# Tap sums by accumulating transfers into device memory, and token products in another order, in a softmax-convolution and mixer kernel

## The chip, the cores and the metric

The kernel runs on one core of one Trainium2 chip. The metric is device time in microseconds (us) of one launch. TensorE is written PE, VectorE DVE, ScalarE ACT, GpSimd POOL and SyncE SP. A change of 0.2% (4.7 us) is about what a measurement of this kernel can tell from none.

## The reference

Two stages in float32. The first is a causal convolution of seven taps whose weights are a softmax per position and head; the second is a mixer with two token products and two channel products for each of eight batches.

```python
w = softmax(weight_gen, axis=-1)                  # (8, 4096, 8 heads, 7 taps), 1e-9 in the divisor
xa[b, s, h, :] = sum_k w[b, s, h, k] * x_pad[b, s + k, h, :]      # d_model 192 = 8 heads x 24
h1 = relu(xa^T @ w_tok1)                          # over the 4096 positions, to 256
u  = xa + (h1 @ w_tok2)^T                         # back to 4096 positions
out = u + relu(u @ w_ch1) @ w_ch2                 # 192 -> 1536 -> 192
```

The weights come in as doubles, and products are kept near float32 by splitting operands in a high and a low part.

## The kernel before

A batch of 4096 positions is cut in eight chunks of 512, each held as 128 partitions x 4 x 192 elements (384 KB); there are 64 chunks, counted m or g. A prologue converts the first weights and does the tap sums of batch 0. The loop at L797 then takes one chunk g at a time through the two channel products, in six steps p. A step is ten matmuls into a `ph` bank (`channel1`, L488), the ReLU on ACT and the low part on DVE (`h`, L499, L500), and, two steps behind, sixteen matmul pairs into `acc` (`channel2`, L504). `ph`, `th` and `up` share two buffers of PSUM (`ps_w`).

Between steps stand the products over tokens. `token1` (L388) sums chunk m of the *next* batch into `h1s`; eight of them make that batch's h1. `token2_half` (L437) runs twice per chunk and gives `ur`, which `columns_of` (L462) transposes on DVE, moves with 24 copies on ACT and splits (L424 to L429) into the operands that the next chunk's first step reads. `store` (L521) adds `acc` to `ur` on DVE and writes the chunk out through POOL's queue.

The tap sums of the batches from 1 on run on DVE beside this. `attention` (L188) does one chunk at a time: product k=0 straight into `xa`, then six products into `pr` (two buffers) and six adds into `xa`. Nine buffers of `xa` (`RING`) keep each sum in SBUF from there until `token2_half`, eight chunks later.

The order of everything is written out when the program is built, by a small planner. It keeps a clock per engine (`at`), holds chains of pending items with costs, and `pump` issues what fits before the next `h` is due. `attention_stream` is one such chain; `token1_ready` and the `if` at L820 to L827 decide which token product stands behind which step. Engines then run in the written order.

```python
        yield "v", cost, first
        yield "v", cost, lambda: one(1)
        for k in range(2, K):
            yield "v", cost, lambda k=k: one(k)
            yield "v", cost, lambda k=k: add(k - 1)
        yield "v", cost, lambda: add(K - 1)
```

Of the kernel before, what the change touches and what calls it, by code (L numbers as in the profile page):

```python
# [21 lines left out]
def mixer_kernel(ctx: ExitStack, tc: tile.TileContext, x, wg, wt1, wt2, wc1, wc2, out):  # L22
# [17 lines left out]
    RING = NCH + 1  # L40
    F1, F2 = 2, 2
    LAG = 2
    SM = 2

# [27 lines left out]
    def load_x(m):  # L72

        b, i = divmod(m, NCH)
        t = p1.tile([P, CT + PAD, D], F32, tag="xt", name="xt", bufs=3)
# [98 lines left out]
    xat, xht = {}, {}  # L174
# [9 lines left out]
    def new_xa(m):  # L184
        xat[m] = p1.tile([P, CT, D], F32, tag="xa", name="xa", bufs=RING)
        return xat[m]

    def attention(m):  # L188
        box = {}
        NE = CT * D  # L190
        cost = 70 + NE * 1.05

        def first():
            box["src"], (box["wn"], box["j"]) = xt.pop(m), wnt.pop(m)
            box["acc"] = new_xa(m)
            mul(box["acc"], 0)

        def mul(dst, k):
            x_k, w = taps(box["src"], box["wn"], box["j"], k, k + 1)
            nc.vector.tensor_mul(  # L200
                dst.rearrange("p t (h g) -> p (t h) g", h=H).rearrange("p (o n) g -> p o n g", o=1), x_k, w)

        def one(k):
            box[k] = late.tile([P, CT, D], F32, tag="pr", name="pr", bufs=2)
            mul(box[k], k)

        def add(k):
            nc.vector.tensor_add(box["acc"], box["acc"], box.pop(k))  # L208
        yield "v", cost, first
        yield "v", cost, lambda: one(1)  # L210
        for k in range(2, K):
            yield "v", cost, lambda k=k: one(k)
            yield "v", cost, lambda k=k: add(k - 1)
        yield "v", cost, lambda: add(K - 1)

    def two_parts(m):
# [12 lines left out]
        yield "n", 0, lambda: ready.append((m, max(at["dve"], at["act"]) + HOP))  # L229
# [14 lines left out]
    def sums(m, prs):  # L244
        acc = new_xa(m)
# [7 lines left out]
        for n in range(2):  # L253
            nc.scalar.copy(acc[:, n * half:(n + 1) * half, :], ps[:, n, 0:half * D])

# [11 lines left out]
    def load_w1(m):  # L267
# [26 lines left out]
    def convert_w2(i):  # L294
# [7 lines left out]
        def last():  # L302
# [3 lines left out]
            nc.gpsimd.dma_start(s2[i], t)  # L306
        yield "a", 950, last

    def load_w2(m):
# [5 lines left out]
        else:  # L315
# [6 lines left out]
            if b == F2:  # L322
                v = v.rearrange("p (k n) -> p k n", k=KR)
                yield from split(t[:, :, 0], t[:, :, 1], v)
                yield "n", 0, lambda: nc.gpsimd.dma_start(s3[i], flat)
# [111 lines left out]
    def token2_half(m, half):  # L437

        b, i = divmod(m, NCH)
        xa, h1, w = xat[m], h1t[b], w2t[m]  # L440
# [18 lines left out]
        if half == 1:  # L459
            del xat[m], w2t[m]  # L460
# [74 lines left out]
    at = {"pe": 0.0, "act": 0.0, "dve": 0.0}  # L535
    HOP = 60
    AFTER = 130
    LOAD = 5000
    SOON = 500
# [4 lines left out]
    FIRST = 0  # L544
# [3 lines left out]
    free = {"acc": 0.0, "u": 0.0}  # L548
    ready = deque()
# [5 lines left out]
    class Chain:  # L555
# [14 lines left out]
        def issue(self):  # L570
            kind, cost, fn = self.item
            fn()
# [12 lines left out]
    def pump(limit):  # L585

        scalar = not state["rush"] and any(c.item is not None and c.item[0] == "u" for c in chains)
        while True:
            best = None
            for c in chains[1:] + chains[:1]:  # L590
# [11 lines left out]
                if kind in "as" and c.wait > max(at["act"], at["pe"]):  # L602
                    continue
# [6 lines left out]
                if kind in "an":  # L610
# [25 lines left out]
    EARLY = 12  # L636
# [11 lines left out]
    def prefetch(m):  # L648

        if m >= NG:  # L650
            return
# [15 lines left out]
    def attention_stream():  # L667
        for m in range(NCH, NG):
            prefetch(m + AHEAD)
            if m % SM == 0 and m > NCH:  # L670
                yield from softmax(m)
            yield "gate", 0, lambda: m - RING <= state["token2"]
            yield from attention(m)
            yield "n", 0, lambda: add_chain(two_parts(m), at["dve"] + HOP)

    with tc.tile_pool(name="pro", bufs=1) as pro:
# [29 lines left out]
        for m in range(NCH):  # L706
            prs = products(m, pro)
            prefetch(m + AHEAD)
# [27 lines left out]
            v_old = v  # L736
        token1_first(NCH - 1, v)
# [13 lines left out]
    stream = chain(softmax(NCH), attention_stream())  # L751
# [5 lines left out]
    run(last, w2_it, islice(stream, EARLY))  # L757
# [20 lines left out]
    def do_token2(m):  # L778
# [10 lines left out]
        state["token2"] = m  # L789
        if NCH <= m + 1 < NG:  # L790
# [6 lines left out]
    for g in range(NG + 1):  # L797
        parts = None if g + 1 < NG else iter(())
        state["rush"] = g == 0
# [70 lines left out]
```

## Time and profile before

| | |
|---|---|
| three runs | 2343.65, 2344.04 (median), 2345.75 us |
| profiled execution | 2343.91 us; its span 2342.1 us |
| busy | PE 2196.7 us (94%), DVE 1842.1 (79%), ACT 1085.0 (46%), POOL 58.4 (2%) |
| tap sums on DVE | 392 products and 336 adds of 128x768 |
| DMA | 244.69 MB, 104 GB/s over the span |

Busy time on PE counts matmuls that overlap, so a busy PE is not PE at its peak. Every chunk ends in one store on POOL (L532), so the distance between two stores is the time of a chunk. The loop over chunks begins at about 130 us; chunks 0 to 7 are batch 0, and so on.

### The profile page before, as it was taken

What the parts mean: (1) busy time and instruction counts of PE and PEld (TensorE: products, weight loads), DVE (VectorE), ACT (ScalarE), POOL (GpSimd) and SP (SyncE); (2) the same over time, 40 slices, a digit from 0 to 9 for tenths busy, and PEclk for the clock granted to TensorE, in tenths of its full rate; (3) what the DMA queues carried; (4) which work ended last, traced back from release to release, by engine and by line L of the source; (5) the groups of instructions that cost most, each with busy time, mean ns of one, the idle gap of its engine ahead of it and who ended that gap; (6) DMA issues with size and microseconds to landing.
All of it is one profiled execution on the core that took longest, in us unless ns stands there. A gap on an engine that the chain in (4) does not pass through costs nothing.

```text
span 2342.1 us, 30675 instructions
## 1 busy us (share of the span) xinstructions
PE 2196.7 (94%) x12256; PEld 1962.0 (84%) x12256; DVE 1842.1 (79%) x2231; ACT 1085.0 (46%) x2265; POOL 58.4 (2%) x104
## 2 busy tenths in 40 slices
PE   7869989999998999999999999999999999999998
PEld 5558878888887888888888888888888888899997
DVE  8889887878876888879887888869887798844443
ACT  4675443544534355345434434444443454344443
POOL 0000000000000000000000000000000000000000
PEclk9989999999999999999999999999999999999999
DMA  7733131223241333313332232332233132211110
GB/s 282 233 133 140 63 106 70 100 97 114 92 156 62 108 113 135 120 64 124 123 107 99 105 122 80 116 112 104 101 107 120 63 124 103 73 55 46 46 42 21
DMA packets 52127, 244.69 MB, mean 104 GB/s; under 512 B 6008, under 2 KB 15736, under 8 KB 38672
## 3 DMA queue, kind: packets, MB, share of 16 engines
q1 hardware_dynamic: 43360, 196.58, 24.3%
q0 software_dynamic: 8624, 46.14, 4.9%
q8 instruction: 97, 1.59, 0.3%
q14 instruction: 46, 0.38, 0.0%
HBM read 192.36 MB, written 50.33 MB: 104 GB/s over the span
## 4 chain that ended last, share of the span: by engine, by line
PE 38%; ACT 19%; DVE 14%; issue 11%; DMA 1%; POOL 0%; POOLq 0%; ACTq 0%; SPq 0%; DVEq 0%
PE ph L496 17%; ACT a_f L476 9%; PE acc L514 9%; ACT c_f L476 4%; PE acc L516 4%; ACT h L499 4%; DVE h L500 3%; DVE xa L208 3%; PE th L397 3%; DVE pr L200 3%; PE up L449 2%; DVE uc L429 1%; PE th L398 1%; DVE a_lo L426 1%; DMA w<-s 1%
## 5 line engine op out<-in xcount | busy, mean ns | idle before, releaser
L514 PE MATMUL acc<-w2s,h 128*128 128x384 f32 x3072 | 902.1, 358 | 0.0
L499 ACT ACTIVATE h<-ph 128x1024 fp32r<-128x1024 f32 x384 | 392.8, 1023 | 1004.4 <-PE ph L496 980.3
L516 PE MATMUL acc<-w2s,h 128*128 128x192 f32 x3072 | 773.5, 252 | 0.0
L500 DVE SCALAR_TENSOR_TENSOR h<-ph,h 128x1024 fp32r<-128x1024 f32 x384 | 468.3, 1220 | 294.3 <-ACT h L499 292.7
L516 PEld LDWEIGHTS acc<-w2s,h 128*128 128x128 f32 x3072 | 591.3, 192 | 16.0
L514 PEld LDWEIGHTS acc<-w2s,h 128*128 128x128 f32 x3072 | 583.3, 190 | 16.0
L496 PE MATMUL ph<-a_hi,w1a_hi 128*128 128x512 f32 x768 | 321.6, 419 | 58.9 <-ACT a_hi L424 33.9
L496 PE MATMUL ph<-uc,w1c_hi 128*128 128x512 f32 x768 | 311.7, 406 | 44.2 <-DVE uc L429 44.2
L200 DVE TENSOR_TENSOR pr<-xt,wn 128x768 f32<-128x768 f32 x336 | 318.2, 952 | 4.1
L208 DVE TENSOR_TENSOR xa<-xa,pr 128x768 f32<-128x768 f32 x336 | 319.7, 952 | 1.0
L496 PE MATMUL ph<-a_lo,w1a_hi 128*128 128x512 f32 x768 | 306.8, 399 | 6.0 <-DVE a_lo L426 6.0
L476 ACT COPY a_f<-t 32x128 f32<-32x128 f32 x1024 | 302.6, 295 | 16.6 <-DVE t L468 5.5
L496 PE MATMUL ph<-a_hi,w1a_lo 128*128 128x512 f32 x768 | 305.6, 398 | 0.0
L496 PE MATMUL ph<-uc,w1c_lo 128*128 128x512 f32 x768 | 305.2, 397 | 0.0
L496 PEld LDWEIGHTS ph<-uc,w1c_hi 128*128 128x128 f32 x768 | 146.6, 191 | 97.6 <-DVE uc L429 49.4
L496 PEld LDWEIGHTS ph<-a_hi,w1a_hi 128*128 128x128 f32 x768 | 146.5, 191 | 87.4 <-ACT a_hi L424 37.3
L496 PEld LDWEIGHTS ph<-a_lo,w1a_hi 128*128 128x128 f32 x768 | 146.6, 191 | 45.8 <-DVE a_lo L426 14.4
L496 PEld LDWEIGHTS ph<-uc,w1c_lo 128*128 128x128 f32 x768 | 147.4, 192 | 30.1
L496 PEld LDWEIGHTS ph<-a_hi,w1a_lo 128*128 128x128 f32 x768 | 148.0, 193 | 16.0
L476 ACT COPY c_f<-t 32x128 f32<-32x128 f32 x512 | 152.0, 297 | 7.4
L528 DVE TENSOR_TENSOR ur<-acc,ur 128x384 f32<-128x384 f32 x256 | 136.2, 553 | 8.3 <-PE acc L516 3.9
L449 PE MATMUL up<-h,w 128*128 128x384 f32 x384 | 116.4, 359 | 0.0
(70 smaller groups left out, 1914.8 us busy)
## 6 DMA issues: line engine op xcount, KB each, us to landing
w<-s SPq DMA_DIRECT2D x80, 1024.0 KB
xt<-in_x_dram SPq DMA_DIRECT2D x56, 960.0 KB
out_dram<-ur POOLq DMA_DIRECT2D x63, 384.0 KB, 4.9
raw<-in_moe_w_tok_dram SPq DMA_DIRECT2D x16, 1024.0 KB
s<-w POOLq DMA_DIRECT2D x16, 1024.0 KB, 4.1
val<-s SPq DMA_DIRECT2D x24, 512.0 KB
wg<-in_weight_gen_dram SPq DMA_DIRECT2D x64, 112.0 KB
s<-val SPq DMA_DIRECT2D x8, 512.0 KB
```

The costliest lines, as they stand in the source:

```text
L200: nc.vector.tensor_mul(dst.rearrange("p t (h g) -> p (t h) g", h=H).rearrange("p (o n) g -> p o n g", o=1), x_k, w)
L208: nc.vector.tensor_add(box["acc"], box["acc"], box.pop(k))
L397: nc.tensor.matmul(th[:, r, 0:2 * D], w[:, c, 0, rs], xh[:, c, :], start=c == 0, stop=False)
L398: nc.tensor.matmul(th[:, r, 0:D], w[:, c, 1, rs], xh[:, c, 0:D], start=False, stop=c == CT - 1)
L449: nc.tensor.matmul(up[:, j, 0:2 * D], w[:, k, 0, cs], h1[:, k, :], start=k == 0, stop=False)
L476: nc.scalar.copy(dst[to:to + Q, :].rearrange("p (c n j) -> p c n j", c=CT, n=NQ)[:, :, n, :], box["t"][n * Q:(n + 1) * Q, :, d, :])
L496: nc.tensor.matmul(ph[:, j, :], w[:, fs], u, start=n == 0, stop=n == len(steps) - 1)
L499: nc.scalar.activation(h[:, :, 0, :], ph, AF.Relu)
L500: nc.vector.scalar_tensor_tensor(h[:, :, 1, :], ph, 0.0, h[:, :, 0, :].bitcast(F32), op0=ALU.max, op1=ALU.subtract)
L514: nc.tensor.matmul(ps[:, 0:2 * D], h[:, j, 0, cs], w2s[:, f, :], start=f == 0, stop=False, **kw)
L516: nc.tensor.matmul(ps[:, 0:D], h[:, j, 1, cs], w2s[:, f, 0:D], start=False, stop=f == NF - 1, **kw)
L528: nc.vector.tensor_add(u[:, t, :], a[:, :, l * D:(l + 1) * D], u[:, t, :])
```

## The change

The six adds per chunk leave DVE. All seven products of a chunk go to `pr` tiles, now eight of them, and each is sent by a DMA on POOL's queue to a tile `xs` in device memory: the first writes, the other six add to what is there (`accum_op`). Two chunks are done in turn, product by product, so that the transfer of one is under way while the other's is issued. The sum is then loaded twice through SP: as `xa` (two buffers) for `token1`, and later as `xb` (two buffers) for `token2_half`. The prologue's sums for chunks 2 to 7 are also written out and loaded again. The 23 later stores of converted weights (to `s2`, `s1`, `s3`) move from POOL's queue to SP's. The x of a pair is loaded when the pair before has had its last product. The planner gets a clock for POOL, and the `if` of the main loop now prefers the halves of token2 to token1.

```diff
-    RING = NCH + 1
+    RUN = NCH + 3
+    PR = 8
...
+    def keep(m):
+        xst[m] = dram.tile([P, CT * D], F32, name=f"xs{m}")
+        return xst[m]
+
+    def load_xa(m):
+
+        xbt[m] = p1.tile([P, CT, D], F32, tag="xb", name="xb", bufs=2)
+        nc.sync.dma_start(xbt[m].rearrange("p t d -> p (t d)"), xst.pop(m))
+
+    def attention(ms):
...
+        def one(m, k):
+            t = late.tile([P, CT, D], F32, tag="pr", name="pr", bufs=PR)
+            x_k, w = taps(xt[m], *wnt[m], k, k + 1)
             nc.vector.tensor_mul(
...
+        def add(m, k):
+            if k == 0:
+                nc.gpsimd.dma_start(keep(m), prt.pop((m, k)))
+            else:
+                nc.gpsimd.dma_start(xst[m], prt.pop((m, k)), accum_op=ALU.add)
+            done[m] = on("pool", ISSUE, at["dve"] + HOP, done.get(m, 0.0)) + ADD
+            pr_free.append(done[m])
+
+        def fetch(m):
+            nc.sync.dma_start(new_xa(m).rearrange("p t d -> p (t d)"), xst[m])
+            xa_at[m] = max(at["pe"], at["dve"]) + FETCH
+            add_chain(two_parts(m), xa_at[m])
...
+        for k in range(K):
+            for m in ms:
+                yield "w", 0, lambda: pr_free.popleft()
+                yield "v", cost, lambda m=m, k=k: one(m, k)
+                yield "n", 0, lambda m=m, k=k: add(m, k)
...
-        xa, h1, w = xat[m], h1t[b], w2t[m]
+        xa, h1, w = xbt[m], h1t[b], w2t[m]
...
-            yield "n", 0, lambda: nc.gpsimd.dma_start(s1[i], flat)
+            yield "n", 0, lambda: nc.sync.dma_start(s1[i], flat)
...
+            yield "gate", 0, lambda: m + SM - 1 - RUN <= state["token2"]
+            yield "w", 0, lambda: x_at[m]
+            yield from attention(range(m, m + SM))
+            if m + SM < NG:
+                yield "t", 0, lambda: load_pair(m + SM)
...
-            if token1_ready() and (p == LAG - 1 or ready[0][0] < g + NCH + ((g + 1) % NCH == 0)):
+            last = (g + 1) % NCH == 0 and (g + 1) // NCH not in h1t and g + 1 < NG
+            if token1_ready() and last:
                 do_token1()
-            elif parts is not None:
+            elif parts is not None and len(halves) > 0:
+                halves.pop()
                 next(parts, None)
-            elif p >= FIRST and g + 1 in w2t and (g + 1) // NCH in h1t \
-                    and max(w_at[0], h1_at[(g + 1) // NCH]) <= at["pe"]:
+            elif parts is None and g + 1 in w2t and (g + 1) // NCH in h1t \
+                    and max(w_at[0], h1_at[(g + 1) // NCH]) <= at["pe"] + 300:
                 parts = do_token2(g + 1)
                 next(parts)
+                halves.append(1)
+            elif token1_ready() and ready[0][0] <= g + NCH:
+                do_token1()
```

**DVE, an inner chunk of batch 3, before.** `ur<-up` is what follows a half of token2, `h1s<-th` what follows token1, `h` closes a step, `ur<-acc` is the store of the chunk before.

```order
L456 TENSOR_TENSOR ur<-up,xa 128x384
L458 TENSOR_TENSOR ur<-up,ur 128x384
L500 SCALAR_TENSOR_TENSOR h<-ph,h 128x2x512
L528 TENSOR_TENSOR ur<-acc,ur 128x384 x4
L406 TENSOR_TENSOR h1s<-th,h1s 128x384
L408 TENSOR_TENSOR h1s<-th,h1s 128x384
L225 TENSOR_TENSOR xh<-xa,xh 128x4x192
L500 SCALAR_TENSOR_TENSOR h<-ph,h 128x2x512
L456 TENSOR_TENSOR ur<-up,xa 128x384
L458 TENSOR_TENSOR ur<-up,ur 128x384
L468 STREAM_TRANSPOSE t<-ur 128x768
```

The same chunk as changed (lines are 27 higher there; `pr<-xt,wn` are tap products, which follow in groups of up to four with no add between):

```order
L483 TENSOR_TENSOR ur<-up,xb 128x384
L485 TENSOR_TENSOR ur<-up,ur 128x384
L527 SCALAR_TENSOR_TENSOR h<-ph,h 128x2x512
L555 TENSOR_TENSOR ur<-acc,ur 128x384 x4
L483 TENSOR_TENSOR ur<-up,xb 128x384
L485 TENSOR_TENSOR ur<-up,ur 128x384
L495 STREAM_TRANSPOSE t<-ur 128x768
L209 TENSOR_TENSOR pr<-xt,wn 128x768
L527 SCALAR_TENSOR_TENSOR h<-ph,h 128x2x512
L209 TENSOR_TENSOR pr<-xt,wn 128x768 x4
L433 TENSOR_TENSOR h1s<-th,h1s 128x384
L435 TENSOR_TENSOR h1s<-th,h1s 128x384
```

The second half of token2 and the transpose stand one step and a token1 earlier. The pair's other nine products follow behind this chunk's next three `h`, three at a time: four `h` stand between the first and the last of the fourteen.

**DVE, the end of a batch (chunk 31), before.** Two token1 stand in it, one with the ReLU of h1 (L385):

```order
L208 TENSOR_TENSOR xa<-xa,pr 128x768
L406 TENSOR_TENSOR h1s<-th,h1s 128x384
L408 TENSOR_TENSOR h1s<-th,h1s 128x384
L385 SCALAR_TENSOR_TENSOR h_9907<-h1s,h_9907 128x2x192
L225 TENSOR_TENSOR xh<-xa,xh 128x4x192
L500 SCALAR_TENSOR_TENSOR h<-ph,h 128x2x512
L528 TENSOR_TENSOR ur<-acc,ur 128x384 x4
L408 TENSOR_TENSOR h1s<-th,h1s 128x384
L500 SCALAR_TENSOR_TENSOR h<-ph,h 128x2x512
L456 TENSOR_TENSOR ur<-up,xa 128x384
L458 TENSOR_TENSOR ur<-up,ur 128x384
L500 SCALAR_TENSOR_TENSOR h<-ph,h 128x2x512
```

As changed:

```order
L247 TENSOR_TENSOR xh<-xa,xh 128x4x192
L433 TENSOR_TENSOR h1s<-th,h1s 128x384
L435 TENSOR_TENSOR h1s<-th,h1s 128x384
L412 SCALAR_TENSOR_TENSOR h_10152<-h1s,h_10152 128x2x192
L527 SCALAR_TENSOR_TENSOR h<-ph,h 128x2x512
L555 TENSOR_TENSOR ur<-acc,ur 128x384 x4
L483 TENSOR_TENSOR ur<-up,xb 128x384
L485 TENSOR_TENSOR ur<-up,ur 128x384
L527 SCALAR_TENSOR_TENSOR h<-ph,h 128x2x512
L483 TENSOR_TENSOR ur<-up,xb 128x384
L485 TENSOR_TENSOR ur<-up,ur 128x384
L495 STREAM_TRANSPOSE t<-ur 128x768
```

The second token1 has left this chunk, and token2 stands one step earlier.

**POOL, a pair of chunks as changed** (before, this queue held a store per chunk here and nothing else). `xs_6513` and `xs_6568` are the two sums.

```order
L559 DMA out_dram<-ur 128x768 x2
L217 DMA xs_6513<-pr 128x768
L217 DMA xs_6568<-pr 128x768
L219 DMA xs_6513<-pr 128x768
L219 DMA xs_6568<-pr 128x768
L219 DMA xs_6513<-pr 128x768
L219 DMA xs_6568<-pr 128x768
L219 DMA xs_6513<-pr 128x768
L219 DMA xs_6568<-pr 128x768
```

Three more such pairs of rows follow. Each row of L219 waits until the one before it on the same sum has landed.

## Rows read from the trace of the kernel before

**Rows 1.** The page: busy us, share of the span and instructions of each engine.

```profile
PE 2196.7 (94%) x12256; PEld 1962.0 (84%) x12256; DVE 1842.1 (79%) x2231; ACT 1085.0 (46%) x2265; POOL 58.4 (2%) x104
```

**Rows 2.** The page: the chain that ended last, by engine.

```profile
PE 38%; ACT 19%; DVE 14%; issue 11%; DMA 1%; POOL 0%; POOLq 0%; ACTq 0%; SPq 0%; DVEq 0%
```

**Rows 3.** Timeline of POOL, one store per chunk: start, us, what [idle before].

```profile
184.84 0.56 POOL L532 DMA_DIRECT2D out_dram<-ur  x1 [15.04 <-PE ph L496]
...
440.20 0.54 POOL L532 DMA_DIRECT2D out_dram<-ur  x1 [27.14 <-DVE ur L528]
...
812.27 0.55 POOL L532 DMA_DIRECT2D out_dram<-ur  x1 [16.52 <-DVE ur L528]
...
1056.03 0.54 POOL L532 DMA_DIRECT2D out_dram<-ur  x1 [32.02 <-DVE ur L528]
...
1255.94 0.54 POOL L532 DMA_DIRECT2D out_dram<-ur  x1 [33.09 <-DVE ur L528]
...
1329.11 0.54 POOL L532 DMA_DIRECT2D out_dram<-ur  x1 [32.03 <-DVE ur L528]
...
2041.58 0.54 POOL L532 DMA_DIRECT2D out_dram<-ur  x1 [32.90 <-DVE ur L528]
...
2164.49 0.54 POOL L532 DMA_DIRECT2D out_dram<-ur  x1 [29.04 <-DVE ur L528]
...
2282.78 0.54 POOL L532 DMA_DIRECT2D out_dram<-ur  x1 [29.03 <-DVE ur L528]
```

**Rows 4.** Waits of PE over the span: us in total, times, longest us.

```profile
PE ph L496 <- DVE uc L429: 44.2, 54, 2.3
PE ph L496 <- ACT a_hi L424: 33.9, 12, 9.7
PE ph L496 <- DVE h L500: 24.6, 28, 7.0
```

**Rows 5.** Windows: us, busy of PE, PEld, DVE, ACT, POOL, PE clock, DMA, GB/s.

```profile
1155.40:1188.90 33.50, 32.50 (x190) 29.43 (x189) 29.10 (x38) 14.97 (x34) 0.57 (x2) 1.00 0.29 104
1280.00:1286.00 6.00, 5.34 (x13) 3.81 (x14) 2.15 (x3) 0.76 (x2) 0.00 (x0) 0.50 0.01 3
```

**Rows 6.** The chain in order of time, one step and a half of token2.

```profile
1155.22 2.33 PE ph L496 x10
...
1159.80 0.20 PE up L449
...
1160.94 2.31 PE ph L496 x10
```

**Rows 7.** Timeline of PE in batch 0: token1, and a half of token2.

```profile
172.93 2.79 PE L415 MATMUL th<-xa,val 128*128 128x192 f32 x16
...
176.17 0.50 PE L496 MATMUL ph<-a_hi,w1a_hi 128*128 128x512 f32 x1 [0.46 <-DVE h L500]
...
180.82 1.49 PE L447 MATMUL up<-h,w 128*128 128x192 f32 x8
...
182.18 0.50 PE L496 MATMUL ph<-a_hi,w1a_hi 128*128 128x512 f32 x1
```

**Rows 8.** Groups by line: busy us, mean ns of one, idle before.

```profile
L200 DVE TENSOR_TENSOR pr<-xt,wn 128x768 f32<-128x768 f32 x336 | 318.2, 952 | 4.1
L208 DVE TENSOR_TENSOR xa<-xa,pr 128x768 f32<-128x768 f32 x336 | 319.7, 952 | 1.0
```

**Rows 9.** DMA queues over the span: packets, MB, share of 16 engines.

```profile
q1 hardware_dynamic: 43360, 196.58, 24.3%
q0 software_dynamic: 8624, 46.14, 4.9%
```

**Rows 10.** The stores of L532: issue on POOL in ns, and landing.

```profile
L532 POOL DMA_DIRECT2D out_dram<-ur x63: 539/539/556, 184.8 to 2311.2; - x63
...
DMA to landing us min/median/max: 2.6/4.9/8.8
```

**Rows 11.** Waits: DVE for the high part in a weight split.

```profile
DVE w L150 <- ACT w L149: 24.0, 12, 5.3
```

More of the change, by code (lines that the diff above doesn't have):

```diff
@@ L74, in load_x @@
         b, i = divmod(m, NCH)
-        t = p1.tile([P, CT + PAD, D], F32, tag="xt", name="xt", bufs=3)
+        if m < NCH and m % 3 == 2:
+            t = pro.tile([P, CT + PAD, D], F32, tag="xt", name="xt")
+        else:
+            t = p1.tile([P, CT + PAD, D], F32, tag="xt", name="xt", bufs=2)
         xt[m] = t
@@ L184, in new_xa @@
     def new_xa(m):
-        xat[m] = p1.tile([P, CT, D], F32, tag="xa", name="xa", bufs=RING)
+        xat[m] = p1.tile([P, CT, D], F32, tag="xa", name="xa", bufs=2)
         return xat[m]
[L188 to L199, printed above, removed]
-            nc.vector.tensor_mul(
[L201 to L214, printed above, removed]
+    def keep(m):
+        xst[m] = dram.tile([P, CT * D], F32, name=f"xs{m}")
+        return xst[m]
@@ L571, in issue @@
             kind, cost, fn = self.item
+            if kind == "w":
+                self.wait = max(self.wait, fn())
+                self.next()
+                return
             fn()
@@ L601, in pump @@
                     continue
-                if kind in "as" and c.wait > max(at["act"], at["pe"]):
+                if kind in "ast" and c.wait > max(at["act"], at["pe"]):
                     continue
@@ L667, in attention_stream, with load_pair @@
     def attention_stream():
[L668 to L674, printed above, removed]
+        for m in range(NCH, NG, SM):
+            yield from softmax(m)
+            if m + SM < NG:
+                yield "t", 0, lambda: load_wg(m + SM)
+            yield "gate", 0, lambda: m + SM - 1 - RUN <= state["token2"]
+            yield "w", 0, lambda: x_at[m]
+            yield from attention(range(m, m + SM))
+            if m + SM < NG:
+                yield "t", 0, lambda: load_pair(m + SM)
+    x_at = {}
+    def load_pair(m):
+        for j in range(SM):
+            load_x(m + j)
+        x_at[m] = max(at["pe"], at["dve"]) + LOAD
     with tc.tile_pool(name="pro", bufs=1) as pro:
@@ L736, in mixer_kernel @@
             v_old = v
+        load_wg(NCH)
+        load_pair(NCH)
         token1_first(NCH - 1, v)
@@ L750, in mixer_kernel @@
             pass
-    stream = chain(softmax(NCH), attention_stream())
+    load_xa(2)
+    stream = attention_stream()
     columns = columns_of(0)
@@ L756, in mixer_kernel @@
     run(columns)
-    run(last, w2_it, islice(stream, EARLY))
+    run(last, w2_it, islice(stream, 6))
     chains.insert(0, Chain(stream))
@@ L799, in mixer_kernel @@
         state["rush"] = g == 0
+        halves = []
         for p in range(NP if g < NG else LAG):
```

45 lines of the change are left out of this document (32 added, 13 removed).

## The prediction

> **What bounds the kernel now.** I read the busy shares first: PE is busy 94% of the span and DVE 79% [rows 1], yet PE holds only 38% of the chain that ended last; ACT, DVE and unexplained issue share the rest [rows 2]. So PE sets the pace but is kept waiting in places. The distance of the stores shows how much. With no tap sums left to do, four chunks take 2282.78 - 2164.49 = 118.3 us, 29.57 each [rows 3], and PE has no gap there. Such a chunk has six steps of 4.58 us and two halves of token2 of 1.14 us [rows 6], 29.8 in all, so 29.57 is PE's floor. Token1 has sixteen matmuls of the shapes of which a half of token2 has eight: 2 x 1.14 = 2.28 us. A chunk with token1 could take 31.85 us. In batches 0 and 1 a half takes 182.18 - 180.82 = 1.36 us, and in batch 0 token1 takes 176.17 - 0.46 - 172.93 = 2.78 us [rows 7].
>
> Against that floor the stores [rows 3] give what is lost:
> - 812.27 to 2041.58, 36 chunks: 1229.3 us against 36 x 31.85 = 1146.6. Lost: **82.7**. Six inner chunks (1056.03 to 1255.94) take 33.32 each, 1.47 over; the two chunks at a batch's end (1255.94 to 1329.11) take 73.17, 9.47 over.
> - 440.20 to 812.27, ten chunks (eight at 29.57 + 0.44 + 2.28 = 32.29, two at 31.85, 322.0): 372.1. Lost: **50.1**.
> - 184.84 to 440.20, seven chunks with eight token1 (7 x 30.01 + 8 x 2.78 = 232.3): 255.4. Lost: **23.1**.
>
> Together 155.9 us. The waits of PE name the cause: the first step of a chunk waits for `uc` (44.2 us, 54 times) and `a_hi` (33.9), the operands that token2's second half sets off, and for `h` (24.6) [rows 4]. In an inner chunk DVE is busy 29.10 of 33.50 us [rows 5], so both the split and `h` queue behind tap work. Behind the long wait at a batch's end PE also runs at a granted clock of 0.50, the lower of its two levels [rows 5].
>
> **The change part by part.** All of it is set against the profiled execution, 2343.91 us with a span of 2342.1; the median of the runs, 2344.04, is the same to 0.01%.
>
> *Adds off DVE.* 336 adds x 952 ns = 319.7 us [rows 8] go; the 392 products stay. DVE falls to 1522 us, per chunk from 29.1 to 23.4. Alone this shortens nothing that PE does; it lets `h` and the split run on time.
>
> *Token order.* In an inner chunk the second half of token2 moves up one step and a token1, 4.58 + 2.28 = 6.9 us, which exceeds the longest wait for `uc` (2.3) [rows 4]. That wait should go, and with it the late step behind it; what is late next is `h` behind a group of three or four products. I leave 0.3 us per inner chunk: 28 x 1.17 = 33 us. At a batch's end one token1 leaves and token2 stands a step earlier; I leave 1.5 of the 9.47: 4 x 8.0 = 32 us. From the first 36 chunks: **65**. In the ten chunks of batch 1 the same waits are joined by the weight splits on DVE, which stay: 70% of 50.1, **35**. In batch 0 the sums start from nothing, so token1 of the first pairs waits for the last landing; I take **10** of 23.1. Sum: 110 us.
>
> *The sums as transfers.* 392 products become 56 writes and 336 accumulating writes of 384 KB, plus 6 writes in the prologue: 398 issues on POOL at 0.54 us [rows 10], 215 us on an engine 2% busy; covered. The trace has no accumulating DMA, so its time from issue to landing, L, is the unknown. A plain store of this size lands in 2.6 to 8.8 us, median 4.9 [rows 10]. The destination has to be read too: queue 0 moved 46.14 MB in 4.9% of the span, 115 us [rows 9], so 402 GB/s and 1.0 us for 384 KB. L then lies between **3.6 and 9.8 us**, and I take **5.9**, from the median, since the new transfers meet weight loads as those stores do. What must hold: seven rounds of L fit in the 63.7 us of a pair (41 at 5.9); and the fourteenth product, which needs the slot of the sixth, finds it free. Four `h` and one token1 stand between first and last product: 4 x 4.58 + 2.28 = 20.6 us. The sixth lands after two products (1.9) and 3 L. That is late from L = 6.2; the `h` behind it may slip one step (4.58) until PE lacks a `ph` buffer, so PE pays from L = 7.8, with 3 L - 23.3 us in each of 28 pairs. At 5.9: nothing.
>
> By the Trainium skill, page "DMA: Bandwidth & Descriptors", section "Anatomy of one DMA", such a transfer takes 2.0 us plus bytes/436 GB/s; 2.9 us is an estimate from it. The median of 4.9 stands against it and decides.
>
> *Engines of the DMA.* Busy now 24.3 + 4.9 = 29% [rows 9]. Added: 398 writes (156.5 MB, 389 us at 402 GB/s), 336 reads of the destination (132 MB, 329 us) and 118 loads of `xa` and `xb` (46.4 MB at 196.58 MB in 569 us, 134 us): 852 us, 36%. Some 66%: not full, but weight loads and sums will meet.
>
> *SP's queue.* A load of `xa` waits on SP for the last landing, and behind it stand weight, x and `xb` loads. The order puts the fetch behind the token1 two chunks earlier, about a chunk ahead of its token1; a chunk of 32 us covers it. If that cover were gone, token1 would wait for L. The 23 moved stores wait on SP for a split, 5.3 us at the longest [rows 11]; the loads behind are due a chunk later: nothing. x for the next pair has some 63.7 - 20.6 = 43 us to land; nothing. The prologue's six stores are POOL's and off PE's path; nothing.
>
> 2343.9 - 110 = **2234 us**. With L at 3.6 and only the 0.3 us per chunk left it comes to 2195.
>
> **The rivals.**
>
> *B, the sums land late.* L between 7.8 and 9.1, since loads and sums bunch: at 8.4, 28 x 1.9 = 53 us is given back: 2287. For it: the 8.8 us landing. Against: the median.
>
> *C, DVE stands behind a slot.* Past L = 9.1 the product that waits for its `pr` slot holds DVE, `h` waits behind it and PE loses more than the order gains: 28 x 3.93 = 110. At the bound of 9.8 the price is 28 x 6.1 = 171, so 2405, and at 11 it is 2508. The pair's seven rounds pass its 63.7 us at the same point. For it: an addition in the transfer may cost more than a second read, which no row bounds. Against: 402 GB/s on queue 0.
>
> The issue on POOL took 539 to 556 ns in all 63 stores [rows 10], with DVE busy 79% of the time. By the Trainium skill, page "SBUF — State Buffer", section "SBUF: two separate sides", some DVE instructions lock GpSimd out while it writes descriptors; the trace shows no such hold, and products (952 ns) behind each issue would bring L from 5.9 to 6.9. I give that 0.02 within C.
>
> *D, weight loads come late.* The gain is real, but each chunk waits for a 1 MB load that shares its engines with the sums: 2 us x 56 = 112 and the time is as before, 2344. Against: 66%, and token products that stand at least three steps behind their load.
>
> **How the numbers follow.** The forecast (2195 to 2285) has 0.62, B 0.13, D 0.06, C 0.19. The range of 2195 to 2350 holds the first three and leaves out C, the bound of 9.8 with it. Faster by over 0.2% is the forecast and B, 0.75; within 0.2%, D, 0.06; slower, C, 0.19.
>
> **What would show it.** Right: no adds on DVE, DVE near 1522 us; stores 31.9 to 32.2 us apart in inner chunks, two chunks at a batch's end near 65 us; PE's waits for `uc` and `a_hi` nearly gone after the first chunks; L near 6. Wrong: long waits of DVE's products for POOL's transfers with `h` right behind (C); PE waiting at token1 or token2 for `w` (D) or `xa`; inner chunks still at 33 us with DVE idle would say that the token order, not DVE, was misread.

## The result: 2353.99 us, and the profile after

The changed kernel takes **2353.99 us** (median of 6 runs, 2350.52 to 2360.92) against 2344.03 of the kernel before beside it: a ratio of 1.0044, 95% interval 1.0029 to 1.0059. It is slower, by 10 us; the forecast was 2234 with a range up to 2350, so 120 us stand between forecast and result.

What was to go is gone. The page's busy times, queues and chain of the changed kernel:

```profile
PE 2188.8 (93%) x12256; PEld 1975.9 (84%) x12256; DVE 1542.6 (66%) x1895; ACT 1086.0 (46%) x2265; POOL 366.3 (16%) x479
...
q0 software_dynamic: 58656, 182.22, 40.8%
q1 hardware_dynamic: 64560, 263.43, 31.7%
...
PE 37%; DMA 22%; DVE 15%; issue 14%; ACT 11%; POOL 0%; SPq 0%; POOLq 0%; DVEq 0%; ACTq 0%
```

DVE fell from 1842.1 us to 1542.6 [rows 1]. But DMA, 1% of the chain before [rows 2], now holds 22% of it, and the DMA engines are 73% busy instead of 29% [rows 9].

A store on POOL now stands behind the adding transfers and no longer marks the end of a chunk; the adds into `ur` on DVE do (L555, the row ahead of each store). Timeline of DVE, start, us, what, at the ends of four stages:

```profile
176.85 2.20 DVE L555 TENSOR_TENSOR ur<-acc,ur 128x384 f32<-128x384 f32 x4
...
459.00 2.20 DVE L555 TENSOR_TENSOR ur<-acc,ur 128x384 f32<-128x384 f32 x4
...
820.81 2.19 DVE L555 TENSOR_TENSOR ur<-acc,ur 128x384 f32<-128x384 f32 x4
...
2054.88 2.19 DVE L555 TENSOR_TENSOR ur<-acc,ur 128x384 f32<-128x384 f32 x4
```

So the seven chunks of batch 0 take 282.1 us, the next ten 361.8, the 36 of which most was expected 1234.1, and the last ten 291.9. Before, by the stores [rows 3], the same stages took 255.4, 372.1 and 1229.3. The 36 chunks gained nothing and batch 0 lost 27 us.

The waits of the changed kernel (PE's, ACT's and DVE's: us in total, times, longest):

```profile
PE ph L523 <- DVE h L527: 57.8, 30, 8.6
...
PE th L442 <- DMA xa<-xs: 13.0, 2, 8.2
...
PE ph L523 <- ACT a_hi L451: 9.7, 1, 9.7
...
PE ph L523 <- DVE uc L456: 3.2, 7, 1.1
...
DVE pr L209 <- DMA xs<-pr: 28.4, 25, 1.9
...
DVE pr L209 <- DMA xt<-in_x_dram: 23.5, 4, 14.2
...
ACT w L153 <- DMA val<-s: 45.5, 6, 10.1
```

`uc` went from 44.2 to 3.2 and `a_hi` from 33.9 to 9.7 [rows 4], as the new order of the token products should make them. The wait for a `pr` slot (rival C) is 28.4 us in 25 places, none longer than 1.9. What else is new are loads that come late: `val` (weights to be split), `xt` and `xa`, and behind them `h`, which went from 24.6 to 57.8 (a late slot delays `h` too). Who was late is in the waits of SP's queue:

```profile
SPq L224 <- DMA xs<-pr: 342.5, 29, 24.2
...
SPq L88 <- POOL xt L86: 124.9, 8, 21.2
```

L224 is the load of a sum, which stands on SP until the last adding transfer has landed, 24.2 us at the longest. L88 is the x of a batch's first chunk; it stands until POOL has filled the margin of that tile with zeros (the memset of L86).

One place for each wait shows what it does. First SP's: the chain in order of time (start, us, what) one chunk before the end of a batch, then the timeline of SP beside it:

```profile
1513.29 8.59 DMA xs<-pr
...
1522.39 4.97 DMA xs<-pr
1527.41 0.33 SPq L224
1527.84 7.11 DMA w<-s
...
1535.09 0.66 PE th L424
```

```profile
1511.39 0.90 SPq L101 DMA_DIRECT2D wg<-in_weight_gen_dram  x2
1527.41 0.33 SPq L224 DMA_DIRECT2D xa<-xs  x1
1527.84 0.42 SPq L310 DMA_DIRECT2D w<-s  x1
```

SP issues nothing from 1512 to 1527: it waits for two adding transfers in a row. Behind it stands the load of token1's weights (L310), which depends on none of this; it goes out at 1527.84, lands 7.11 us later, and only then can token1 begin; PE stands 3.2 us for it. That chunk took 39.6 us (1505.58 to 1545.20).

The wait for the memset, some 610 us earlier, in the timelines of POOL and then SP:

```profile
898.29 0.86 POOL L219 DMA_DIRECT2D xs<-pr  x1 [2.12 <-DMA xs<-pr]
898.83 1.05 POOL L86 MEMSET xt<- 2x1152 f32 x1
```

```profile
899.91 0.25 SPq L88 DMA_DIRECT2D xt<-in_x_dram  x1
...
902.40 0.79 SPq L345 DMA_DIRECT2D val<-s  x1
```

The memset takes 1 us, but stands on POOL behind adding transfers, seven of them since 881, each of which may go out only when the one before it on its sum has landed. SP's load of x waits 20.2 us for it, the `val` load behind it is late, ACT waits 10.1 us for `val` (885 to 935), and PE 8.6 us for `h`.

The wait for a slot, on the chain, in a chunk at a batch's end:

```profile
1294.99 7.31 DMA xs<-pr x2
...
1302.32 0.02 DVEq L209
...
1304.40 1.13 DVE h L527
```

Two transfers land; only then is the `pr` tile free that DVE's next product needs, and `h` stands behind that product. Followed over the whole span, the chain goes from a landing into a product's slot some twenty times (about 260 us of transfers), and into the load of a sum six times (90 us). Such a share tells where the chain runs, not what a shorter wait would give back.

### The profile page after: what moved, and what is told of

Its sections match the earlier page's. It is cut to its first block, busy times and chain, and to the rows that moved or that the text cites. A ratio compares the mean times of both kernels' runs of the same rounds, so it can differ in the third digit from the quotient of the medians.

```text
span 2353.9 us, 31326 instructions
## 1 busy us (share of the span) xinstructions
PE 2188.8 (93%) x12256; PEld 1975.9 (84%) x12256; DVE 1542.6 (66%) x1895; ACT 1086.0 (46%) x2265; POOL 366.3 (16%) x479
## 3 DMA queue, kind: packets, MB, share of 16 engines
q0 software_dynamic: 58656, 182.22, 40.8%
## 4 chain that ended last, share of the span: by engine, by line
PE 37%; DMA 22%; DVE 15%; issue 14%; ACT 11%; POOL 0%; SPq 0%; POOLq 0%; DVEq 0%; ACTq 0%
PE ph L523 18%; DMA xs<-pr 16%; PE acc L541 9%; ACT a_f L503 5%; PE acc L543 4%; DVE h L527 4%; DVE pr L209 3%; ACT c_f L503 2%; DMA val<-s 2%; ACT h L526 2%; DVE ur L555 2%; DMA xt<-in_x_dram 2%; PE up L476 2%; PE th L424 1%; DVE prk L262 1%
## 5 line engine op out<-in xcount | busy, mean ns | idle before, releaser
L527 DVE SCALAR_TENSOR_TENSOR h<-ph,h 128x1024 fp32r<-128x1024 f32 x384 | 467.9, 1220 | 378.6 <-ACT h L526 376.9
L219 POOL DMA_DIRECT2D xs<-pr x336 | 288.5, 859 | 905.9 <-DMA xs<-pr 380.4
L523 PE MATMUL ph<-a_hi,w1a_hi 128*128 128x512 f32 x768 | 323.1, 421 | 97.3 <-DVE h L527 57.8
L209 DVE TENSOR_TENSOR pr<-xt,wn 128x768 f32<-128x768 f32 x392 | 355.3, 948 | 52.1 <-DMA xs<-pr 28.4
L523 PE MATMUL ph<-uc,w1c_hi 128*128 128x512 f32 x768 | 306.4, 399 | 3.2 <-DVE uc L456 3.2
L559 POOL DMA_DIRECT2D out_dram<-ur x63 | 42.1, 669 | 779.9 <-DVE ur L555 763.9
L555 DVE TENSOR_TENSOR ur<-acc,ur 128x384 f32<-128x384 f32 x256 | 136.0, 552 | 8.5 <-PE acc L543 4.0
```

Source lines behind the costliest of these rows:

```text
L209: nc.vector.tensor_mul(t.rearrange("p t (h g) -> p (t h) g", h=H).rearrange("p (o n) g -> p o n g", o=1), x_k, w)
L219: nc.gpsimd.dma_start(xst[m], prt.pop((m, k)), accum_op=ALU.add)
L523: nc.tensor.matmul(ph[:, j, :], w[:, fs], u, start=n == 0, stop=n == len(steps) - 1)
L527: nc.vector.scalar_tensor_tensor(h[:, :, 1, :], ph, 0.0, h[:, :, 0, :].bitcast(F32), op0=ALU.max, op1=ALU.subtract)
L555: nc.vector.tensor_add(u[:, t, :], a[:, :, l * D:(l + 1) * D], u[:, t, :])
L559: nc.gpsimd.dma_start(rows, u)
```

## The experiments

Times are medians; ratios are to the kernel before, run beside each, with the 95% interval. Two theories were set against each other from the first results on: **C**, that DVE's products stand behind `pr` slots, and **Q**, that the in-order queue of SP (and of POOL) holds loads that are due; later a third, **E**, that the DMA engines, full of adding transfers, make every load late. In the expectations 1a is Q, and 1b is E or C. In e3, e4, e5, e9, e12 and e15 taps are left out of the sums that the kernel goes on with; they show times only.

| run | us | ratio |
|---|---|---|
| the change | 2353.99 | 1.0044 [1.0029, 1.0059] |
| e1 order alone | 2269.18 | 0.9681 [0.9665, 0.9697] |
| e2 sums alone | 2559.97 | 1.0923 [1.0884, 1.0962] |
| e3 no adding transfers | 2232.35 | 0.9522 [0.9507, 0.9536] |
| e4 plain writes instead | 2233.26 | 0.9526 [0.9512, 0.9540] |
| e5 adds aside | 2279.17 | 0.9724 [0.9710, 0.9739] |
| e6 sum loaded by POOL | 2344.31 | 1.0004 [0.9991, 1.0018] |
| e7 planner's cost 5500 | 2290.63 | 0.9783 [0.9755, 0.9811] |
| e8 three groups of taps | 2255.97 | 0.9629 [0.9614, 0.9643] |
| e10 two groups | 2269.40 | 0.9678 [0.9662, 0.9694] |
| e11 four groups | 2253.18 | 0.9610 [0.9596, 0.9625] |
| e9 aside, from a still tile | 2274.35 | 0.9702 [0.9688, 0.9717] |
| e12 aside, memset on DVE | 2254.29 | 0.9622 [0.9608, 0.9637] |
| e13 memset on DVE | 2335.74 | 0.9976 [0.9960, 0.9992] |
| e14 4 groups, memset on DVE | 2255.77 | 0.9621 [0.9605, 0.9638] |
| e15 plain and more plain writes | 2339.94 | 0.9988 [0.9975, 1.0000] |
| e16 memset on DVE, cost 5500 | 2252.54 | 0.9620 [0.9599, 0.9642] |
| e17 and the sum loaded 8 us later | **2245.41** | 0.9584 [0.9567, 0.9601] |
| e18 4 groups, both | 2251.09 | 0.9609 [0.9593, 0.9624] |

### The two halves of the change (e1, e2)

e1 is the kernel before with the new `if` of the main loop; e2 the changed kernel with the old one.

> The kernel before, with the changed if of the main loop alone (halves of token2 ahead of token1); sums stay on DVE. If the token order is worth what the prediction gave it and does not need a free DVE, the waits of PE for uc and a_hi go and the time falls by 30 to 60 us, to 2285 to 2315. If the order only pays together with a lighter DVE, it stays within 10 us of 2344, or rises since the split and h still queue behind tap work.

> The changed kernel with the old if of the main loop: sums by transfers, old token order. If the transfers themselves cost time (theory 1: full DMA engines, late landings, late loads), this is slower than the changed kernel, 2380 to 2420, since it lacks the order's gain. If the loss comes from the new order standing badly against the pairs (theory 2), it is faster than the changed kernel, 2310 to 2340.

The order alone gives 75 us, more than the 30 to 60 expected, with all adds still on DVE, which is then 81% busy; PE's wait for `uc` is 3.2 us there too. So the order did not need a lighter DVE. The sums as transfers, in the old order, cost 216 us, far more than either theory gave: the loads of the sums hold SP for 456.5 us, and `a_hi` comes late, 229.7 us in 24 waits.

### What the adding transfers cost (e3, e4)

e3 leaves the six adding transfers of a chunk out, e4 makes them plain writes:

```diff
-                nc.gpsimd.dma_start(xst[m], prt.pop((m, k)), accum_op=ALU.add)
+                prt.pop((m, k))
```

```diff
-                nc.gpsimd.dma_start(xst[m], prt.pop((m, k)), accum_op=ALU.add)
+                nc.gpsimd.dma_start(xst[m], prt.pop((m, k)))
```

> The changed kernel without the six adding transfers of a chunk (336 in all); only the product of tap 0 is written and loaded, so the sums lack six taps. Products, token order and loads stay. Theory 1 (transfers cost the gain): about 2234, the forecast, with inner chunks at 32 us and a start without stalls. Theory 2 (groups of products in front of h, order): still 2320 or more. A start that stays 25 us late here would be due to the loads, not the sums.

> The changed kernel with plain writes in place of the adding ones: same issues, bytes written and waits, but no add, so the sum is the product of the last tap alone. If it is the work of adding in the DMA engines that hurts (2.5 us of all 16 engines per adding transfer, worked out from the queue's share, against 1.0 for a plain one), the time lies near that without adds, 2240 to 2280. If it is the number of transfers and their chain of waits, it stays at 2330 to 2355.

Without them the forecast's time is there, 2232; with as many plain writes too, 2233. So 336 plain transfers, with 542 ns of issue on POOL each, cost nothing that can be measured, and the loads, which both versions have, leave the forecast's time: what costs is that the transfers add, **121 us**. (The change also takes the x tiles from three buffers to two, which its description leaves out; e3 and e4 have two as well.) What an adding transfer is beside a plain one, in the changed kernel and then in e4 (issue on POOL in ns; landing):

```profile
L219 POOL DMA_DIRECT2D xs<-pr x336: 841/859/902, 143.0 to 2004.3; - x168
...
DMA to landing us min/median/max: 4.4/5.5/11.8
```

```profile
L219 POOL DMA_DIRECT2D xs<-pr x336: 542/542/556, 141.4 to 1868.0; - x168
...
DMA to landing us min/median/max: 2.6/2.9/9.3
...
q0 software_dynamic: 37152, 182.22, 20.8%
...
SPq L224 <- DMA xs<-pr: 102.9, 19, 15.5
```

The same bytes take 20.8% of e4's 2231.1 us on queue 0, 464 us, and 40.8% of 2353.9, 960 us, as adds: 496 / 336 = 1.5 us more of all 16 engines each. Part of the loss shows as PE's own busy time, 2188.8 us against 2151.6 in e4 for the same 12256 matmuls: its mean granted clock is 0.971 in the changed kernel and 0.993 in e4.

### Slots, the load of the sum, or the engines (e5, e9, e6)

In e5 the first product is written to `xs` as before, and the six others go to a second tensor that nothing loads, so the load of the sum waits for one plain write only. e9 does that from one tile that never changes, so that no product can wait for a slot. e6 is the changed kernel with L224 issued on POOL. The edits of e5, e9 (against e5) and e6:

```diff
+            elif k == 1:
+                xqt[m] = dram.tile([P, CT * D], F32, name=f"xq{m}")
+                nc.gpsimd.dma_start(xqt[m], prt.pop((m, k)))
             else:
-                nc.gpsimd.dma_start(xst[m], prt.pop((m, k)), accum_op=ALU.add)
+                nc.gpsimd.dma_start(xqt[m], prt.pop((m, k)), accum_op=ALU.add)
```

```diff
-                nc.gpsimd.dma_start(xqt[m], prt.pop((m, k)), accum_op=ALU.add)
+                prt.pop((m, k))
+                nc.gpsimd.dma_start(xqt[m], const_t[0], accum_op=ALU.add)
```

```diff
-            nc.sync.dma_start(new_xa(m).rearrange("p t d -> p (t d)"), xst[m])
+            nc.gpsimd.dma_start(new_xa(m).rearrange("p t d -> p (t d)"), xst[m])
```

> The changed kernel with its adds going to a second tensor that nothing loads: tap 0 is written to xs, which is loaded as before, tap 1 is written and taps 2 to 6 are added to the other (280 adding transfers instead of 336). So the sums lack six taps. The load of the DMA engines and the waits for product slots stay nearly as they are; only the load of xa on SP no longer waits for the last add. Theory 1a (the load of xa stands on SP for the last landing, and the loads behind it come late): 2235 to 2260. Theory 1b (the DMA engines are too full, all loads come late, or products wait for slots): 2310 to 2345.

> As the run with the adds aside (2279), but the six transfers of taps 1 to 6 all read one tile that is filled once, so no product waits for a slot to come free, while the engines do the same adds; the sums lack six taps again. If what is left over the plain writes there (46 us) is DVE standing for a slot with h behind it (the slot part of rival C), this falls to 2235 to 2245. If it is the full DMA engines making x, weight and store transfers late (rival D's mechanism), it stays at 2265 to 2285.

> The changed kernel with the load of xa issued on POOL's queue, where the adds are, instead of SP's. Theory 1a: SP no longer stands for a landing, weight and x loads go out on time; the price is that POOL stands instead, so adds and stores behind the load come a few us later: 2250 to 2300. Theory 1b: 2340 to 2360, since neither the engines' load nor the slots change.

e5 brings 75 us of the 121 back and ends between the two theories, though the DMA engines are nearly as full (0.81 from 1300 to 1600 against 0.84; 56 of the adds have become plain writes). But it doesn't remove SP's wait alone. DVE's wait for slots, which I expected to stay, went from 28.4 us to 3.3:

```profile
DVE pr L209 <- DMA xq<-pr: 3.3, 5, 1.0
```

So the 75 us belong to both waits together, and e9, which gives a further 5 with overlapping intervals, could take away only the slot waits that were left. C isn't ruled out by it. e6 takes the wait off SP and leaves the slots:

```profile
POOL xa L224 <- DMA xs<-pr: 58.9, 24, 6.6
...
DVE pr L209 <- DMA xs<-pr: 27.0, 19, 2.4
```

It gains 10 us, where Q gave at least 54. POOL now stands for the landings, but 58.9 us in all against SP's 342.5, so that the moved wait can hardly be the whole answer; the memset (122.1 us of SP's waits) and the slots stay as they were. This run speaks against SP's wait as the main cost. Of e5's rest, the waits of SP hold one candidate:

```profile
SPq L88 <- POOL xt L86: 115.8, 8, 20.8
```

### The memset, or full engines (e12, e13, e15)

e12 is e5 and e13 the changed kernel with one line changed; e15 is e4 with nine more plain writes per chunk, of the same tiles, to tensors that nothing loads.

```diff
-        nc.gpsimd.memset(t[0:2, 0:PAD, :], 0.0)
+        nc.vector.memset(t[0:2, 0:PAD, :], 0.0)
```

```diff
-                nc.gpsimd.dma_start(xst[m], prt.pop((m, k)))
+                t = prt.pop((m, k))
+                nc.gpsimd.dma_start(xst[m], t)
+                for j in range(1 + k % 2):
...
+                    nc.gpsimd.dma_start(xqt[m % 4, k, j], t)
```

> The kernel with the adding transfers aside (the second to seventh products of a chunk go to a second tensor in device memory that nothing loads, so the sums are not used), with one more edit: the small fill of zeros before the first x of a batch moves from POOL to DVE. Theory Q (POOL's fill stands behind the adding transfers, the load of x on SP waits 16 to 21 us for it, and the weight loads behind it come late): most of the 41 to 46 us that the adding transfers cost with the load of the sums out of their way goes; 2235 to 2255 us. Theory E (the DMA engines, busy 0.81 of the time, make every load late): nothing changes, 2265 to 2285 us.

> The changed kernel with one edit: the fill of zeros before the first x of a batch moves from POOL to DVE. Theory Q: the 16 to 21 us waits of SP for POOL's fill go (125 us in 8 of them), those for the last landing of a sum stay (342 us in 29); the time falls by 25 to 45 us, to 2310 to 2330. Theory E: 2345 to 2355, no change.

> The kernel with plain writes in place of the adding ones (the output's sums are then the last product alone), and nine more plain writes per chunk that go to tensors nothing loads: 504 more writes of 384 KB, about as much time of the DMA engines as the adding transfers took over plain ones (some 500 us of all sixteen), but none that a load waits for. Theory E (full engines make the loads late): 2265 to 2285 us. Theory Q (it is the waits in the queues of SP and POOL): 2233 to 2250, where more than 2233 comes from POOL, which has 504 more issues of 0.54 us ahead of the fills and stores.

e12 recovers 25 of the 46 us between e5 and e4. The 36 chunks take as long in e4 as in e12 (timelines of DVE, first e4, then e12):

```profile
748.91 2.19 DVE L555 TENSOR_TENSOR ur<-acc,ur 128x384 f32<-128x384 f32 x4
...
1932.02 2.20 DVE L555 TENSOR_TENSOR ur<-acc,ur 128x384 f32<-128x384 f32 x4
```

```profile
771.18 2.19 DVE L558 TENSOR_TENSOR ur<-acc,ur 128x384 f32<-128x384 f32 x4
...
1954.71 2.20 DVE L558 TENSOR_TENSOR ur<-acc,ur 128x384 f32<-128x384 f32 x4
```

1183.1 and 1183.5 us: there 280 adding transfers cost nothing, with the engines 0.79 busy from 1300 to 1600 against 0.58 in e4. What is left lies in batch 0, where the pipeline of sums starts: by the same rows 255.1 us against 236.0. e13 gains 18 us, less than the 25 named by Q and more than E allowed; SP stands longer for the sums there (411.5 us in 35 waits).

e15 came out where neither theory put it: without one addition, 107 us slower than e4, as slow as the kernel before and only 14 us faster than the change. Its rows (landing of the `xs` writes; waits of SP, where L229 is the load of the sum):

```profile
DMA to landing us min/median/max: 2.6/5.3/13.5
```

```profile
SPq L229 <- DMA xs<-pr: 318.7, 28, 19.8
...
SPq L88 <- POOL xt L86: 120.4, 8, 20.8
```

The extra writes stand in the same queue as the ones that count, which land as late as adds do (5.3 us, adds 5.5), and SP stands nearly as long as in the changed kernel. So a late landing costs time whether it adds or not. Whether the landings are late because the engines are full or because more transfers stand ahead in one queue, e15 doesn't part. Full engines alone don't explain the loss (e12).

### The same transfers, with loads in another order (e7, e16, e17)

```diff
-    ISSUE, ADD = 1000, 2500
+    ISSUE, ADD = 860, 5500
...
-            add_chain(iter([("gate", 0, lambda: state["token1"] >= m - 2), ("t", 0, lambda: fetch(m))]), done[m])
+            add_chain(iter([("gate", 0, lambda: state["token1"] >= m - 2), ("t", 0, lambda: fetch(m))]), done[m] + 8000)
```

e7 is the first edit, e16 the first with the memset on DVE, e17 both edits with it. Every adding transfer stays.

> The changed kernel with the planner told what an adding transfer takes here: 860 ns of issue and 5500 ns to landing instead of 1000 and 2500. It changes only the written order: products further apart, the load of xa later in SP's queue. Theory 1a: SP stands less, 2270 to 2310. Theory 1b: no gain from order, 2335 to 2360.

> The changed kernel, all six adding transfers kept, with the fill of zeros on DVE and the planner told that an issue on POOL takes 860 ns and an adding transfer 5500 (it had 1000 and 2500). The DMA engines carry the same work as in the changed kernel. Theory Q (waits in SP's queue): the two edits gained 18 and 63 us alone and should add up to 2265 to 2280. Theory E (full engines): no better than the larger one alone, 2285 to 2295.

> The same with one more edit: the load of a sum is put on SP's queue another 8 us later in the planner's time than the last landing that it expects. Theory Q: SP stands for the landing in few places (below 100 us in all against 342 in the changed kernel); 2245 to 2265, near the 2254 that the kernel with adds aside and the fill on DVE took. Theory E: 2285 to 2295, or more if the later load makes token1 wait.

2290.6 (as Q said), 2252.5 (below the range of either theory) and **2245.4** us (the lower edge of Q's). The trace's durations in place of the 1000 and 2500 ns give 63 us; with the memset on DVE and the later load, 109 of the 121 us are gone, with all 336 adding transfers and DMA engines as busy as before (0.84 in both rows; windows of the changed kernel, then of e17: us, PE, PEld, DVE, ACT, POOL, clock, DMA, GB/s):

```profile
1300.00:1600.00 300.00, 286.22 (x1639) 261.40 (x1638) 203.54 (x265) 136.85 (x303) 58.15 (x74) 0.98 0.84 213
```

```profile
1300.00:1600.00 300.00, 296.12 (x1731) 272.38 (x1731) 209.58 (x271) 145.63 (x329) 55.80 (x72) 0.99 0.84 220
```

The waits of e17 that answer to those above, and the timeline of its SP in the chunk that took 39.6 us above (1421.90 to 1455.19 here, 33.3 us):

```profile
PE ph L523 <- DVE h L527: 17.0, 17, 2.3
...
DVE pr L209 <- DMA xs<-pr: 12.3, 13, 2.4
...
DVE pr L209 <- DMA xt<-in_x_dram: 0.8, 1, 0.8
...
ACT w L153 <- DMA val<-s: 4.1, 2, 3.8
...
SPq L224 <- DMA xs<-pr: 315.3, 31, 17.6
```

```profile
1430.10 0.33 SPq L310 DMA_DIRECT2D w<-s  x1
1445.35 3.15 SPq L224 DMA_DIRECT2D xa<-xs  x2
```

The late loads are gone (`val` 45.5 to 4.1, `xt` 23.5 to 0.8), and `h` with them. But my "below 100 us" for SP's wait missed: it still stands 315 us for landings. What changed is who stands behind: here the weights of token1 (L310) go out 15 us ahead of the load of the sum, not behind it. The sum of a queue's waits is not its price. The first edit also moves DVE's products, and the slot waits go with it. e7's, over the whole span, while SP still stands 279.3 us:

```profile
DVE pr L209 <- DMA xs<-pr: 8.9, 8, 2.3
```

Side by side, in the 36 chunks of which most was expected (waits in us; how often in brackets):

| run | 36 chunks, us | SP for a landing | DVE for a slot | memset |
|---|---|---|---|---|
| the change | 1234.1 | 218.0 (18) | 18.4 (17) | POOL |
| e13 | 1225.4 | 258.6 (22) | 20.8 (16) | DVE |
| e15 | 1224.3 | 204.0 (18) | 9.6 (15) | POOL |
| e6 | 1222.6 | none; POOL 24.7 (12) | 16.2 (12) | POOL |
| e7 | 1199.0 | 223.0 (18) | 1.4 (2) | POOL |
| e5 | 1196.0 | none | 0.9 (2) | POOL |
| e12 | 1183.5 | none | 0.2 (1) | DVE |
| e4 | 1183.1 | 55.6 (12) | none | POOL |
| e16 | 1177.3 | 269.4 (22) | 1.7 (4) | DVE |
| e17 | 1176.1 | 270.6 (22) | 1.6 (4) | DVE |

The versions above 1220 us are those in which DVE stands for slots, though not in proportion (e15); how long SP stands says nothing of the time: e16 is e13 with the planner's new constants, SP stands as long, and 48 us go. That makes rival C's wait a suspect for much of the loss. It isn't proof, since the same constants also send loads out ahead of the one that stands, and 18 us of DVE's waiting alone are less than 48. A version that frees slots and leaves the loads where they are was not run.

### Fewer adding transfers (e8, e10, e11, e14, e18)

Here DVE adds within groups of taps and only the groups are added in transfers, with the planner's 860 and 5500: e8 has groups 01, 23, 456, e10 012, 3456, and e11 01, 23, 45, 6 (six, four and six `pr` tiles). e14 is e11 with the memset on DVE, e18 that with the load 6 us later.

```diff
-        for k in range(K):
+        for ks in GROUPS:
             for m in ms:
                 yield "w", 0, lambda: pr_free.popleft()
-                yield "v", cost, lambda m=m, k=k: one(m, k)
+                yield "v", cost, lambda m=m, k=ks[0]: one(m, k)
+                for k in ks[1:]:
+                    yield "v", cost, lambda m=m, k=k: more(m, k)
+                    yield "v", cost, lambda m=m, k=k, to=ks[0]: nc.vector.tensor_add(prt[m, to], prt[m, to], prt.pop((m, k)))
```

> A version between the two: taps 0 and 1, 2 and 3, 4 to 6 are summed on DVE (four adds per chunk), and three transfers per chunk go out, one write and two adds, so 112 adding transfers instead of 336; six product slots, and the planner with 860 and 5500 ns. Both theories: the chain of landings per pair falls from seven to three rounds and the engines' share by a quarter, so 2245 to 2265, below the order alone with all adds on DVE (2269) if transfers at this number are free; above 2269 if any adding transfer costs more than the add on DVE that it replaces.

> Taps 0 to 2 and 3 to 6 summed on DVE (five adds per chunk), one write and one adding transfer per chunk, 56 in all; four slots. If each add on DVE costs PE more than an adding transfer that is well covered, 2258 to 2268, between three groups (2256) and the order alone (2269). If even few adding transfers cost, 2245 to 2255.

> Taps 0+1, 2+3, 4+5 and 6: three adds on DVE and one write with three adding transfers per chunk, 168 in all. If transfers at this number are still covered, one DVE add less per chunk gives 2245 to 2253. If the last landing again comes too late for the load of xa or the engines fill, 2260 or more.

> Four groups of taps (0 and 1, 2 and 3, 4 and 5, 6), added on DVE within a group, three adding transfers per chunk, with the fill of zeros on DVE. Theory Q: less to gain than with six adding transfers, since POOL's queue is shorter; 2235 to 2250 us against 2253 with the fill on POOL. Theory E: 2250 to 2256, no change.

> Four groups of taps with three adding transfers per chunk, the fill on DVE, and the load of a sum 6 us later. Theory Q: what SP still stood for the landing goes, 2235 to 2250 against 2253 to 2256 for the four groups. Theory E: 2250 to 2260.

All lie between 2251 and 2269. The memset and the later load gain nothing measurable there, so that e14 and e18 came out as E said and not as Q did; with half the adding transfers the memset had cost little from the start (e11's SP waits 11.6 us for it, against 124.9). The lowest median of a version that computes the whole result is e17's, with every add in a transfer, though its interval touches those of e16 and e18. Against the order alone (e1), its transfers are worth 24 us.

## Why the prediction was wrong, point by point

- **Adds off DVE, token order: right in sum.** DVE 1542.6 (forecast 1522); `uc` and `a_hi` waits nearly gone. The sum of 110 us is what e3 and e4 show, 2232 and 2233 against 2234. Its parts are not, by e4: 36 chunks 46.2 (forecast 65), ten chunks 34.9 (35), batch 0 19.4 (10), and some 10 us before the first chunk's end and after the last's, for which I had no term. That they make 110 together is luck. And I took the lighter DVE as the condition of the order; e1 shows 75 of the 110 without it.
- **L, the time of an adding transfer: right by luck, and used as one number.** The median is 5.5 us against 5.9 taken. But I added 1.0 for reading the destination to a plain 4.9; the plain writes of e4 take 2.9, and adding brings 2.6 more. And the price of the slots, "At 5.9: nothing", was worked out for one L. Landings run from 4.4 to 11.8 us, beyond the bound of 9.8, and DVE stood for a slot 25 times, 28.4 us. (Past the bound, C's 2508 should read 2506 by its own formula, and the low end of 2195 is 2196.)
- **POOL's queue: mis-sized, and one thing not seen.** An issue took 859 ns, not 540. It was "covered" for the transfers themselves (e4). What stood behind them was overlooked: the memset of L86, which the diff does not touch, and which the move of 336 transfers put behind waits for landings. It cost 18 us (e13) to 25 (e12 against e5).
- **The step that failed: every wait for a landing was taken as covered.** For the slots it was "At 5.9: nothing"; for SP's queue "a chunk of 32 us covers it", for the load of a sum that waits there, and "x for the next pair has some 63.7 - 20.6 = 43 us to land; nothing". In e4, where the transfers land in 2.9 us at the median, SP stands 102.9 us for sums instead of 342.5, DVE never for a slot, and the 121 us are gone. I asked whether the *sum* would be in time, and it nearly was (`xa` made PE wait 13.0 us). I did name what stood behind the waiting load, but gave each of them a chunk of slack that it didn't have: weights and x wait up to 24.2 us for a landing that they have nothing to do with, then need their own 7 us. 75 of the 121 us hang on SP's wait and the slots together (e5), 18 to 25 on the memset ahead of SP's queue, and some 20 stay in batch 0 (e12, where DVE still stands 13.8 us for slots, nearly all of it there). How the 75 divide between SP and the slots is open; e6, and e13 beside e16, speak for the slots.
- **The moved stores** stood on SP up to 15.5 us (L308, for a split on DVE), not 5.3; no cost of it shows, since they stand as long in e4 (15.8).
- **Why products and loads stood there so early** was in the diff and not priced: the planner places both by 2500 ns per adding transfer, where my own L was 5.9. With 5500 written there the cost falls by 63 us (e7), with the memset on DVE by 101 (e16).
- **Engines of the DMA: 66% forecast, 73% found**, since an add takes some 2.5 us of the engines (e4's 464 us for 182.22 MB are 1.0 per 384 KB, and 1.5 more), where I had 1.0 for the write and 1.0 for the read. With products and loads in good order this costs little: e17 has 75%.
- **The rivals.** In time D, 2344, and C, from 2344 up, both come near. D named late weight loads, but as a matter of shared engines. The loads were issued late, and they also took longer: the `w` load above 7.11 us, where the chain of the kernel before has 4.77 for one. No run parts the two. C's mechanism, a product that holds DVE for a slot with `h` behind it, is there too, at a median L far below the 9.1 from which C counted it.

By the Trainium skill, page "DMA: Bandwidth & Descriptors", section "Rules for kernel authors", a DMA that reads what an earlier one wrote has to wait for the earlier one's semaphore before it is issued; by its section "Anatomy of one DMA — SWDGE (gpsimd) path" such a wait stands on the issuing sequencer, not in the DMA engine. The rows of SP above agree: nothing is issued from 1512 to 1527. The estimate of 2.9 us for a plain transfer of this size that the prediction worked out from that section's formula, and set aside for a median of 4.9, is the median of e4's plain writes (2.9); for adds, 5.5, the section has no figure.

Open: how the 75 us divide between SP's wait and the slots; why landings come late (full engines, or one queue); and the 12 us that e17 still stands above e4, which lie in batch 0 (254.9 us against 236.0; its 36 chunks, 1176.1, are 7 us shorter). No run here was made for that stage.

## What to carry to other kernels

When work goes from an engine to transfers, list for every in-order queue what stands behind the new waits, and give each of those its own due time: a load that waits for a landing holds loads that depend on nothing. Price a wait by the spread of the landings, not by their median. Where a planner places products and loads, its constant for the transfer has to be the measured one. An experiment meant to take one wait away should be checked for the others: here it took two. A fill or another small operation on the queue that gets the transfers is part of the change, though the diff doesn't show it.

## What the runs showed of the hardware

- An adding transfer of 384 KB from SBUF to device memory takes 859 ns to issue on POOL (a plain one 542), lands in 5.5 us at the median (2.9 for a plain one in e4), takes 1.5 us more of all 16 engines, and 64 more packets ((58656 - 37152) / 336).
- 504 more plain writes in POOL's queue brought the median landing of the plain writes there from 2.9 to 5.3 us (e15), as late as adds.
- A store on POOL right behind such an issue took up to 907 ns (L559; 556 at most before [rows 10]).
